# Moving the product of two weight matrices behind the attention, with its loads on another queue

## The chip, the cores and the metric

The kernel runs on one core of a Trainium2 chip. The time is the device time of one execution in microseconds (us), lower is better: the median of 3 executions of the kernel before is 733.92 us (733.58 to 734.43).

## The reference, cut to what matters

```python
# q, k, v: (4, 12, 448, 64); x below: (1792, 768)
scores = q @ k.T / sqrt(64) - log(448)
x = sigmoid(scores) @ v                            # heads joined to 768 columns
h = max(x @ w1, x @ w2, x @ w3)                    # three 768 x 768 matrices
x = h @ w_out                                      # 768 x 768
h = x @ w_in                                       # 768 x 1024
s = h * softmax(h)
out = layernorm(s) * g_ln @ w_out2                 # 1024 x 768
```

All in float32; the weights come as 64-bit floats.

## The kernel before, in words

**Precision.** TensorE works in a reduced float32 format, so most operands are split in a high part (a cast) and a low part (what the cast left, helper `rest`, L56), and each product is three matmuls: high x high, high x low, low x high. Only the product of attention weights and v (L300) takes plain float32.

**Folding two matrices.** There is nothing between `w_out` (wo) and `w_in` (wi), so the kernel computes W = wo x wi itself (`gen_w`, L242): 12 groups of 18 matmuls, 512 columns each, into a PSUM tile `pw`. ACT and DVE split each result into a tile `ws`, and GpSimd's queue (POOL) writes it to DRAM (`w_d`, L258), from where it is read back late (`wf`, L399).

**Preparing weights.** One unit is 128 x 768 doubles. `load_next` (L132) loads it into one of two `raw` buffers, on SyncE's queue (SP). `prepare` (L163) turns it into float32 (ACT L147, DVE L150 and L153), asks for the next load, then makes the high part (ACT, L51) and the low part (DVE, L56). wi lies whole in SBUF (`wip`); units of wo and w1 to w3 go through a ring of three slots (`ring`). The program text puts these operations in a list of background work, and `run_bg(n)` emits the next n of them. 11 units are needed before W can be finished that far (`first`: 8 of wi, 3 of wo).

**Attention.** 24 pairs of heads. For a pair: `load_qk` and `load_v` (SP), `prep_qk` splits q and k (four DVE operations), `scores` makes four blocks c = 0..3 (six matmuls each, two at a time in the two halves of the array's rows, L281, then one sigmoid on ACT, L289), and `attend` multiplies the four blocks with v (L300; the trace counts two matmuls for each in the text) and splits the result into `xh` (ACT) and `xl` (DVE). The text runs `attend` one pair behind `scores`.

**Order.** Only TensorE's order is that of the text. For ACT, DVE, POOL and SP a planner in the compiler walks the program in its own modelled time and lets each engine take the earliest instruction of the text whose inputs and buffers are then free; the resulting order is fixed, and each engine runs it strictly in sequence.

**W between the pairs.** From pair 4 on, `fill(9)` puts half a group of W behind each pair (L329), in a single PSUM bank (`ps_f`); what is left runs after the last pair (L332). PSUM has eight banks: six for scores, one for `av`, one for `pw`.

**What follows.** `layer1` (tile `pg`, 72 groups of 18 matmuls, 448 columns: 1296), then by 128 tokens `layer2` with W (tile `h`, L426, 512 columns, 504 matmuls) and `output` (tile `po`, L502, 384 columns, 672 matmuls).

**Where the tiles lie.** SBUF is laid out from the left (const, ring, wip, apool and, once these are closed, h, w2, wf, hsplit) and from the right (x, raw, tp). In the program of before the bytes within a partition are: ring 1728 and wi 20160 (both multiples of 64), hh 161472, wf 112320 and w2 63168 (multiples of 64 too), kt 81344 and qt 89536 (multiples of 64); xh 143328 and, for `output`, lh 206816 lie 32 past a multiple of 64. The second tiles of each kind keep these remainders.

Of the kernel before, what the change touches and what calls it, by code (L numbers as in the profile page):

```python
# [7 lines left out]
F32 = mybir.dt.float32  # L8
F32R = mybir.dt.float32r
# [4 lines left out]
PSUM = bass.MemoryType.PSUM  # L14
DRAM = bass.MemoryType.DRAM

P = 128
B, H, S, D = 4, 12, 448, 64
SX = S + D
# [9 lines left out]
U = 768  # L29
NG = 3 * FC  # L30
RAWS = 2
WARM = 4


def sigmoid_attention_max_moe_solu_ln(tc, q, k, v, w123, wo, wi, w2, g, out):
# [13 lines left out]
    def copy(eng, dst, src):  # L49
        if eng is act:  # L50
            act.copy(dst, src)  # L51
        else:
            eng.tensor_copy(dst, src)
# [4 lines left out]
    def open_pool(name, bufs, side="left", space=None):  # L58
        kw = dict(name=name, bufs=bufs, side=side)
        if space is not None:  # L60
            kw["space"] = space
        cm = tc.tile_pool(**kw)
        return cm, cm.__enter__()

    def shut(*cms):
        for cm in cms:
            cm.__exit__(None, None, None)
# [2 lines left out]
    order.__enter__()  # L70
    dr_cm, dram = open_pool("dram", 1, space=DRAM)
    c_cm, const = open_pool("const", 1)
    r_cm, ring = open_pool("ring", 3)
    x_cms, xps = [], []
    for b in reversed(range(B)):
        cm, p = open_pool(f"xp{b}", 1, side="right")
# [2 lines left out]
    raw_cm, rawp = open_pool("rawp", 2, side="right")  # L79
    wi_cm, wip = open_pool("wip", 1)  # L80
    a_cm, apool = open_pool("apool", 2)
    ps1 = [open_pool("ps_sc", 3, space=PSUM), open_pool("ps_av", 1, space=PSUM), open_pool("ps_f", 1, space=PSUM)]
    ps_sc, ps_av, ps_f = (p for _, p in ps1)

    ident = const.tile([P, P], F32, name="ident")
    bias_s = const.tile([P, 1], F32, name="bias_s")
# [10 lines left out]
    def run_bg(n=1):  # L97
        while n > 0 and bg:
            if next(bg[0], "end") == "end":
                bg.popleft()  # L100
            else:
                n -= 1
# [20 lines left out]
    def source(key):  # L123
        if key[0] == "wi":
            return wi[key[1], key[2]]
        if key[0] == "wo":
            return wo[key[1]]
        if key[0] == "w2":
            return w2[key[1]]
        return w123[key[1]]  # L130

    def load_next():  # L132
        i = state["load"]
        if i >= len(stream):
            return
        state["load"] += 1
        key = stream[i]
        t = rawp.tile([P, U, 2], I32, tag="raw", name=f"raw{i}", bufs=RAWS)
        sp.dma_start(out=t, in_=source(key).rearrange("p (n t) -> p n t", t=2))
        raws[key] = t  # L140

    def to_f32(raw, y):
# [20 lines left out]
    def prepare(key):  # L163

        raw = raws.pop(key)
        y = rawp.tile([P, U], F32, tag="y", name="y_" + "_".join(map(str, key)), bufs=2)
        for op in to_f32(raw, y):
            op()
            yield
        load_next()  # L170
        if key[0] == "wi":
            _, n, i = key
            if i % 2 == 0:
                wis[(n, i // 2)] = [wip.tile([P, 2 * U], F32R, name=f"wi{p}{n}_{i}") for p in ("h", "l")]
            hi, lo = (t[:, (i % 2) * U : (i % 2 + 1) * U] for t in wis[(n, i // 2)])
        elif key[0] == "w2":
            kc = key[1]
            act.activation(y, y, AF.Copy, scale=g_sb[:, kc : kc + 1])
            yield
            hi, lo = w2t["h"][:, kc], w2t["l"][:, kc]  # L180
        else:
            slot = ring.tile([P, 2, U], F32R, tag="ring", name="r_" + "_".join(map(str, key)))
            slots[key] = slot
            hi, lo = slot[:, 0], slot[:, 1]
        copy(act, hi, y)
        yield
        rest(dve, lo, y, hi)
        ready.add(key)
        yield
# [16 lines left out]
    def load_qk(pr):  # L206
        if pr >= NP:
            return
        kr = apool.tile([P, SX], F32, tag="kr", name=f"kr{pr}", bufs=1)
        qr = apool.tile([P, S], F32, tag="qr", name=f"qr{pr}", bufs=1)  # L210
        sp.dma_start(out=kr, in_=k[pr])
        sp.dma_start(out=qr, in_=q[pr])
        qk_raw[pr] = (qr, kr)

    def load_v(pr):
        if pr >= NP:
            return
        vr = apool.tile([P, 2, 4, D], F32, tag="vr", name=f"vr{pr}", bufs=2)
        sp.dma_start(out=vr, in_=v[pr])
        v_ops[pr] = vr  # L220

    def prep_qk(pr):
        if pr >= NP:
            return
        qr, kr = qk_raw.pop(pr)
        kt = apool.tile([P, 2, SX], F32R, tag="kt", name=f"kt{pr}")
        qt = apool.tile([P, 2, S], F32R, tag="qt", name=f"qt{pr}")
        qk_ops[pr] = (qt, kt)
        copy(dve, kt[:, 0], kr)
        copy(dve, qt[:, 0], qr)  # L230
        rest(dve, kt[:, 1], kr, kt[:, 0])
        rest(dve, qt[:, 1], qr, qt[:, 0])
        load_qk(pr + 1)


    def group(ps, terms):
# [5 lines left out]
    def gen_w():  # L242
        for n, fc in groups:
            need(("wo", fc))
            for i in range(4):
                need(("wi", n, i))
            wo_s = slots[("wo", fc)]
            ps = ps_f.tile([P, 512], F32, tag="f", name=f"pw{n}_{fc}")
            terms = []
            for kc in range(KC):  # L250
                lh, ll = (wo_s[:, i, kc * P : (kc + 1) * P] for i in range(2))
                rh, rl = (t[:, (kc % 3) * 512 : (kc % 3 + 1) * 512] for t in wis[(n, kc // 3)])
                terms += [(lh, rh), (lh, rl), (ll, rh)]
            yield from group(ps, terms)
            s = wip.tile([P, 2, 512], F32R, tag="ws", name=f"ws{n}_{fc}", bufs=1)
            copy(act, s[:, 0], ps)
            rest(dve, s[:, 1], ps, s[:, 0])
            pool.dma_start(out=w_d[:, fc, :, n * 512 : (n + 1) * 512], in_=s.bitcast(F32))  # L258
            if n == 1:
                slots.pop(("wo", fc))  # L260
                queue_unit(stream[len(first) + fc])

    filler = gen_w()

    def fill(n):
        for _ in range(n):
            if next(filler, "end") == "end":
                return


    xs_hi, xs_lo, hts = {}, {}, {}
    weights = {}
# [1 line left out]
    def scores(pr, c):  # L274
        qt, kt = qk_ops[pr]
        sc = ps_sc.tile([P, 2, 512], F32, tag="sc", name=f"sc{pr}_{c}")
        terms = ((0, 0), (0, 1), (1, 0))
        for t, (x, y) in enumerate(terms):
            for j in range(2):
                rows = slice(j * D, (j + 1) * D)  # L280
                pe.matmul(  # L281
                    sc[:, j, :S],
                    lhsT=kt[rows, x, c * P : (c + 1) * P],
                    rhs=qt[rows, y],
                    start=(t == 0),
                    stop=(t == len(terms) - 1),
                )
        sf = apool.tile([P, 2, S], F32, tag="sf", name=f"sf{pr}_{c}", bufs=7)
        act.activation(sf, sc[:, :, :S], AF.Sigmoid, bias=bias_s, scale=1.0 / math.sqrt(D))  # L289
        weights[(pr, c)] = sf  # L290

    def attend(pr):

        b, hp = divmod(pr, NPAIR)
        vr = v_ops.pop(pr)
        pa = ps_av.tile([P, 512], F32, tag="av", name=f"av{pr}")
        for c in range(4):
            sf = weights.pop((pr, c))
            for j in range(2):
                pe.matmul(pa[j * D : (j + 1) * D, :S], lhsT=vr[:, j, c], rhs=sf[:, j], start=(c == 0), stop=(c == 3))  # L300
        if hp == 0:
            xs_hi[b] = xps[b].tile([P, KC, S], F32R, name=f"xh{b}")
            xs_lo[b] = xps[b].tile([P, KC, S], F32R, name=f"xl{b}")
        copy(act, xs_hi[b][:, hp], pa[:, :S])
        rest(dve, xs_lo[b][:, hp], pa[:, :S], xs_hi[b][:, hp])
        load_v(pr + 2)


    act.preload_act_table_set("sigmoid_and_others")
    load_qk(0)  # L310
    load_v(0)
    load_next()
    load_next()
    prep_qk(0)
    load_v(1)
    sp.dma_start(out=g_sb, in_=g)
    for key in first:
        queue_unit(key)
    for pr in range(NP + 1):
        if pr < NP:  # L320
            for c in range(4):
                scores(pr, c)
                if c == 1:
                    prep_qk(pr + 1)
                run_bg(1)
        if pr > 0:
            attend(pr - 1)
            run_bg(2)
        if WARM <= pr < NP:  # L329
            fill(9)  # L330
        run_bg(2)
    while next(filler, "end") != "end":  # L332
        pass
    for cm, _ in reversed(ps1):
        shut(cm)
    shut(a_cm, wi_cm)


    h_cm, hpool = open_pool("hpool", 1)
    w2_cm, w2p = open_pool("w2p", 1)  # L340
    psg_cm, ps_g = open_pool("ps_g", 4, space=PSUM)
    w2t["h"], w2t["l"] = (w2p.tile([P, K2, DM], F32R, name=f"w2{p}") for p in "hl")
    hts = [hpool.tile([P, NT], F32, name=f"h{f}") for f in range(FC)]
    tick = [0]
# [231 lines left out]
```

## Time and profile before

| | before |
|---|---|
| median of 3 executions | 733.92 us |
| the profiled execution | 736.76 us, its span 734.8 us |
| PE busy in the span | 708.0 us (96%) |
| DVE busy | 318.7 us (43%) |
| ACT busy | 264.9 us (36%) |
| mean granted clock of TensorE | 0.995 |
| moved by DMA | 80.81 MB |

The span runs from the first to the last instruction of the profiled execution. A busy PE is not yet a PE at its peak: matmuls overlap, and one that waits or runs at a slow pace still counts as busy. So the pace from start to start is read beside the busy time. W and attention end at 228.97 us of the span, `layer1` at 496.81 us, and the rest belongs to `layer2` and `output`.

### The profile page before, as it was taken

To read this page: it belongs to the slowest core of one execution; us is meant where nothing else is said; L and a number is where in the kernel's file an instruction comes from. 1 tells how busy PE (TensorE), PEld (TensorE's weight loads), DVE (VectorE), ACT (ScalarE), POOL (GpSimd) and SP (SyncE) were. 2 spreads that over 40 slices of the span, in tenths; PEclk is the share of its full clock that TensorE was granted. 3 is DMA by queue.
4 is the path that set the end of the run, shared out by engine and by line. 5 is a ranking of instruction groups with operands and counts; after the bars stand their busy time and mean duration, and the time that the engine had idled before them with its cause. 6 is when DMAs were issued, how large, how long until landed. Compare 5 with 4: busy or idle time off the path is not lost.

```text
span 734.8 us, 9063 instructions
## 1 busy us (share of the span) xinstructions
PE 708.0 (96%) x3664; PEld 574.9 (78%) x3664; DVE 318.7 (43%) x578; ACT 264.9 (36%) x428; POOL 9.6 (1%) x19
## 2 busy tenths in 40 slices
PE   5887999999999999999999999999999999999998
PEld 3344555555557999999999999997999999999997
DVE  4875345343422243533532131214954455555540
ACT  5875566555652123333330110101422223232221
POOL 0000000000000000000000000000000000000000
PEclk9999999999999999999999999999999999999999
DMA  7887344453324122333231000710132222222231
GB/s 242 280 269 258 118 154 154 124 176 118 128 72 144 43 87 87 128 106 110 86 114 60 1 0 1 295 48 1 58 114 94 98 90 79 79 79 79 79 101 44
DMA packets 29706, 80.81 MB, mean 110 GB/s; under 512 B 3424, under 2 KB 12896, under 8 KB 28896
## 3 DMA queue, kind: packets, MB, share of 16 engines
q1 hardware_dynamic: 27936, 73.94, 29.9%
q0 software_dynamic: 1728, 6.29, 2.2%
q8 instruction: 29, 0.48, 0.3%
q14 instruction: 13, 0.11, 0.0%
HBM read 62.13 MB, written 18.09 MB: 109 GB/s over the span
## 4 chain that ended last, share of the span: by engine, by line
PE 89%; DMA 5%; ACT 4%; issue 1%; DVE 0%; SPq 0%; ACTq 0%
PE pg L239 36%; PE po L502 16%; PE h L426 16%; PE av L300 8%; PE pw L239 7%; PE sc L281 6%; DMA raw<-in_wo 3%; DMA raw<-in_wi 2%; ACT sf L289 2%; ACT y_wo L147 1%; ACT ws L51 0%; ACT y_wi L147 0%; ACT wih L51 0%; PE pt L486 0%; DVE wil L56 0%
## 5 line engine op out<-in xcount | busy, mean ns | idle before, releaser
L239 PE MATMUL pg<-xh,r_w 128*128 128x448 f32 x864 | 249.0, 369 | 0.0
L239 PEld LDWEIGHTS pg<-xh,r_w 128*128 128x128 f32 x864 | 162.4, 188 | 16.3
L239 PE MATMUL pg<-xl,r_w 128*128 128x448 f32 x432 | 159.4, 369 | 0.0
L426 PE MATMUL h<-wf,hh 128*128 128x512 f32 x336 | 103.9, 390 | 0.8 <-issue 0.8
L289 ACT ACTIVATE sf<-sc,bias_s 128x896 f32<-128x896 f32 x96 | 92.0, 1007 | 28.6 <-PE sc L281 25.3
L281 PE MATMUL sc<-qt,kt 64*128 64x448 f32 x576 | 75.4, 399 | 21.0 <-ACT sf L289 14.1
L239 PEld LDWEIGHTS pg<-xl,r_w 128*128 128x128 f32 x432 | 81.2, 188 | 7.9
L281 PEld LDWEIGHTS sc<-qt,kt 64*128 64x128 f32 x576 | 53.6, 196 | 42.8 <-ACT sf L289 26.3
L300 PE MATMUL av<-sf,vr 128*64 128x448 f32 x384 | 80.2, 561 | 0.0
L502 PE MATMUL po<-w2h,lh 128*128 128x384 f32 x224 | 75.4, 336 | 0.0
L502 PE MATMUL po<-w2h,ll 128*128 128x384 f32 x224 | 75.3, 336 | 0.0
L502 PE MATMUL po<-w2l,lh 128*128 128x384 f32 x224 | 75.3, 336 | 0.0
L364 DVE TENSOR_TENSOR h<-pg,h 128x448 f32<-128x448 f32 x48 | 29.9, 624 | 102.9 <-PE pg L239 102.9
L426 PEld LDWEIGHTS h<-wf,hh 128*128 128x128 f32 x336 | 62.8, 188 | 13.4 <-issue 1.1
L426 PE MATMUL h<-wf,hl 128*128 128x512 f32 x168 | 65.6, 390 | 0.0
L300 PEld LDWEIGHTS av<-sf,vr 128*64 128x64 f32 x384 | 26.1, 140 | 43.1 <-issue 42.2
L438 DVE TENSOR_REDUCE st<-h 128x1 f32<-128x1024 f32 x14 | 17.1, 1223 | 85.1 <-PE h L426 85.1
L239 PE MATMUL pw<-wih,r_wo 128*128 128x512 f32 x144 | 50.8, 409 | 1.4 <-DVE ws L56 1.4
L51 ACT CAST hh<-h 128x128 fp32r<-128x128 f32 x84 | 18.1, 295 | 93.6 <-PE h L426 86.7
L51 ACT CAST r_w<-y_w 128x768 fp32r<-128x768 f32 x18 | 15.1, 839 | 93.3 <-PE pg L239 93.3
L239 PEld LDWEIGHTS pw<-wih,r_wo 128*128 128x128 f32 x144 | 27.0, 187 | 21.9 <-issue 11.3
L502 PEld LDWEIGHTS po<-w2l,lh 128*128 128x128 f32 x224 | 42.1, 188 | 0.6
(65 smaller groups left out, 606.7 us busy)
## 6 DMA issues: line engine op xcount, KB each, us to landing
raw<-in_w SPq DMA_DIRECT2D x26, 768.0 KB, 4.3
kr<-in_k SPq DMA_DIRECT2D x24, 256.0 KB, 2.8
vr<-in_v SPq DMA_DIRECT2D x24, 256.0 KB, 3.2
raw<-in_wi SPq DMA_DIRECT2D x8, 768.0 KB, 5.8
w_d<-ws POOLq DMA_DIRECT2D x12, 512.0 KB, 3.2
wf<-w_d SPq DMA_DIRECT2D x6, 1024.0 KB, 10.0
u_d<-ub SPq DMA_DIRECT2D x12, 512.0 KB, 3.0
ut<-u_d SPq DMA_DIRECT2D x48, 128.0 KB, 3.1
```

The source lines that it names most:

```text
L51: act.copy(dst, src)
L147: act.activation(y, raw.bitcast(F32)[:, :, 1], AF.Prelu, scale=2.0**-112, alpha=2.0**32)
L239: pe.matmul(ps, lhsT=l, rhs=r, start=(i == 0), stop=(i == n - 1))
L281: pe.matmul(sc[:, j, :S], lhsT=kt[rows, x, c * P : (c + 1) * P], rhs=qt[rows, y], start=(t == 0), stop=(t == len(terms) - 1),)
L289: act.activation(sf, sc[:, :, :S], AF.Sigmoid, bias=bias_s, scale=1.0 / math.sqrt(D))
L300: pe.matmul(pa[j * D : (j + 1) * D, :S], lhsT=vr[:, j, c], rhs=sf[:, j], start=(c == 0), stop=(c == 3))
L364: dve.tensor_tensor(out=hv, in0=ps[:, :S], in1=hv, op=ALU.max)
L426: pe.matmul(ps[:, n], lhsT=l, rhs=r, start=(f == 0 and i == 0), stop=(f == FC - 1 and i == 2))
L438: dve.tensor_reduce(out=nmax, in_=ps, axis=AX.XY, op=ALU.max, negate=True)
L502: pe.matmul(ps[:, :hw], lhsT=l, rhs=r, start=(kc == 0 and i == 0), stop=(kc == K2 - 1 and i == 2))
```

## The change

W's groups leave the attention: `fill` and `WARM` go, and all 12 groups run after the last pair, each in one of four PSUM banks (the pool `ps_g` that `layer1` uses too), with two `ws` buffers. Every fourth matmul emits one background operation there.

The freed bank goes to `av`, which has two. `attend` is cut by blocks: behind the scores of a pair come blocks 2 and 3 of the pair before and blocks 0 and 1 of this pair.

The raw weights are loaded from POOL's queue, and the text asks for the first two with pair 1 (`load_next`) and emits three background operations for each pair from pair 2 on. The high part of wi, wo and w1 to w3 is cast by DVE in place of ACT.

q and k have two buffers each and are loaded two pairs ahead, v has three; the buffers for attention weights (`sf`) go from 7 to 6. A pad of 32 bytes in `const` shifts everything that is laid out from the left by 32 bytes.

```diff
     c_cm, const = open_pool("const", 1)
+    const.tile([P, 8], F32, name="pad")
...
-    ps1 = [open_pool("ps_sc", 3, space=PSUM), open_pool("ps_av", 1, space=PSUM), open_pool("ps_f", 1, space=PSUM)]
+    ps1 = [open_pool("ps_sc", 3, space=PSUM), open_pool("ps_av", 2, space=PSUM)]
...
-        sp.dma_start(out=t, in_=source(key).rearrange("p (n t) -> p n t", t=2))
+        pool.dma_start(out=t, in_=source(key).rearrange("p (n t) -> p n t", t=2))
...
-        copy(act, hi, y)
+        copy(act if key[0] == "w2" else dve, hi, y)
...
-        kr = apool.tile([P, SX], F32, tag="kr", name=f"kr{pr}", bufs=1)
-        qr = apool.tile([P, S], F32, tag="qr", name=f"qr{pr}", bufs=1)
+        kr = apool.tile([P, SX], F32, tag="kr", name=f"kr{pr}", bufs=2)
+        qr = apool.tile([P, S], F32, tag="qr", name=f"qr{pr}", bufs=2)
...
-        load_qk(pr + 1)
+        load_qk(pr + 2)
...
-            s = wip.tile([P, 2, 512], F32R, tag="ws", name=f"ws{n}_{fc}", bufs=1)
+            s = wsp.tile([P, 2, 512], F32R, tag="ws", name=f"ws{n}_{fc}", bufs=2)
...
+    for pr in range(2):
+        load_qk(pr)
+        load_v(pr)
+    load_v(2)
     prep_qk(0)
...
+    for pr in range(NP):
+        if pr == 1:
+            load_next()
+            load_next()
+        for c in range(4):
+            scores(pr, c)
+            if c == 1:
+                prep_qk(pr + 1)
+        if pr > 1:
+            run_bg(1)
         if pr > 0:
-            attend(pr - 1)
-            run_bg(2)
-        if WARM <= pr < NP:
-            fill(9)
-        run_bg(2)
-    while next(filler, "end") != "end":
-        pass
+            attend(pr - 1, 2)
+            attend(pr - 1, 3)
+        if pr > 1:
+            run_bg(1)
+        attend(pr, 0)
+        attend(pr, 1)
+        if pr > 1:
+            run_bg(1)
+    attend(NP - 1, 2)
+    attend(NP - 1, 3)
+    run_bg(1 << 20)
...
+    psg_cm, ps_g = open_pool("ps_g", 4, space=PSUM)
+    ws_cm, wsp = open_pool("wsp", 2)
+    for i, _ in enumerate(gen_w()):
+        if i % 4 == 3:
+            run_bg()
+    shut(ws_cm, wi_cm)
```

## Rows read from the trace of the kernel before

**Rows 1.** Stretches: length; busy PE, PEld, DVE, ACT, POOL (count); clock; DMA share, GB/s.
```profile
4.98:73.84 68.86, 53.94 (x291) 29.71 (x291) 48.26 (x77) 48.18 (x59) 0.84 (x1) 0.95 0.80 269
73.84:207.45 133.61, 132.50 (x787) 76.46 (x786) 53.15 (x96) 79.90 (x96) 5.84 (x8) 1.00 0.43 139
...
228.97:496.81 267.84, 267.84 (x1296) 243.30 (x1295) 87.60 (x128) 63.71 (x92) 0.74 (x1) 1.00 0.24 85
```

**Rows 2.** The chain that ended last, share of the span by line.
```profile
by line: PE pg L239 36.4%; PE po L502 15.9%; PE h L426 15.7%; PE av L300 8.3%; PE pw L239 6.8%; PE sc L281 5.8%; DMA raw<-in_wo 2.8%; DMA raw<-in_wi 2.5%; ACT sf L289 1.9%; issue 0.6%; ACT y_wo L147 0.5%; ACT ws L51 0.5%; ACT y_wi L147 0.4%
```

**Rows 3.** Waits from 4.98 to 73.84 us: total us, times, longest.
```profile
PEld sc L281 <- ACT sf L289: 19.8, 11, 4.3
PE sc L281 <- ACT sf L289: 13.0, 6, 3.9
ACT y_wi L147 <- DMA raw<-in_wi: 10.6, 3, 7.2
```

**Rows 4.** ACT's first two entries in the order of time: start, us.
```profile
9.27 0.89 ACT L147 ACTIVATE y_wi<-raw 128x768 f32<-128x768 f32 x1 [7.25 <-DMA raw<-in_wi]
10.06 1.90 ACT L289 ACTIVATE sf<-sc,bias_s 128x896 f32<-128x896 f32 x2
```

**Rows 5.** The chain in order of time, pieces of it: start us, us, what.
```profile
124.13 2.78 PE sc L281 x24
126.91 3.16 PE av L300 x16
130.07 2.27 PE pw L239 x9
132.34 2.85 PE sc L281 x24
...
182.35 0.59 ACT ws L51
...
223.23 0.59 ACT ws L51
...
223.85 0.70 DVE ws L56
...
224.59 4.37 PE pw L239 x18
228.97 267.84 PE pg L239 x1296
...
523.26 8.33 PE po L502 x48
531.59 8.21 PE h L426 x36
```

**Rows 6.** Tile `raw`, whole run: duration min/median/max ns, first to last start.
```profile
L147 ACT ACTIVATE y_w<-raw x26: 890/902/921, 117.9 to 424.7; 128x768 f32<-128x768 f32 x26
```

**Rows 7.** Groups of instructions from 4.98 to 73.84 us: busy us, mean ns, idle before.
```profile
L53 DVE CAST kt<-kr 128x512 fp32r<-128x512 f32 x8 | 3.4, 425 | 2.4 <-DMA kr<-in_k 1.5 <-PE sc L281 0.8
...
L289 ACT ACTIVATE sf<-sc,bias_s 128x896 f32<-128x896 f32 x28 | 27.2, 1007 | 2.5 <-PE av L300 1.4 <-PE sc L281 1.0
...
L51 ACT CAST wih<-y_wi 128x768 fp32r<-128x768 f32 x8 | 6.7, 833 | 0.9 <-DVE y_wi L153 0.9
```

**Rows 8.** What SP's queue waited for, up to 74 us: total us, times, longest.
```profile
SPq L211 <- DVE kt L56: 15.0, 8, 2.6
```

**Rows 9.** Tile `w_d`, whole run: POOL's issues, and its DMAs from issue to landing.
```profile
L258 POOL DMA_DIRECT2D w_d<-ws x12: 727/727/844, 66.1 to 230.7; - x12
...
DMA to landing us min/median/max: 3.1/3.2/15.8
```

**Rows 10.** Tile `raw` up to 74 us: its DMAs from issue to landing.
```profile
DMA to landing us min/median/max: 4.2/5.8/8.5
```

**Rows 11.** PE in order of time, pair 23: two score matmuls that start together, twice.
```profile
208.10 0.37 PE L281 MATMUL sc<-qt,kt 64*128 64x448 f32 x2
...
208.93 0.37 PE L281 MATMUL sc<-qt,kt 64*128 64x448 f32 x2
```

More of the change, by code (lines that the diff above doesn't have):

```diff
@@ L31 @@
 RAWS = 2
-WARM = 4
 def sigmoid_attention_max_moe_solu_ln(tc, q, k, v, w123, wo, wi, w2, g, out):
@@ L81, in sigmoid_attention_max_moe_solu_ln @@
     a_cm, apool = open_pool("apool", 2)
-    ps1 = [open_pool("ps_sc", 3, space=PSUM), open_pool("ps_av", 1, space=PSUM), open_pool("ps_f", 1, space=PSUM)]
-    ps_sc, ps_av, ps_f = (p for _, p in ps1)
+    ps1 = [open_pool("ps_sc", 3, space=PSUM), open_pool("ps_av", 2, space=PSUM)]
+    ps_sc, ps_av = (p for _, p in ps1)
     ident = const.tile([P, P], F32, name="ident")
@@ L217, in load_v @@
             return
-        vr = apool.tile([P, 2, 4, D], F32, tag="vr", name=f"vr{pr}", bufs=2)
+        vr = apool.tile([P, 2, 4, D], F32, tag="vr", name=f"vr{pr}", bufs=3)
         sp.dma_start(out=vr, in_=v[pr])
@@ L247, in gen_w @@
             wo_s = slots[("wo", fc)]
-            ps = ps_f.tile([P, 512], F32, tag="f", name=f"pw{n}_{fc}")
+            ps = ps_g.tile([P, 512], F32, tag="g", name=f"pw{n}_{fc}")
             terms = []
@@ L261, in gen_w @@
                 queue_unit(stream[len(first) + fc])
[L263 to L268, printed above, removed]
     xs_hi, xs_lo, hts = {}, {}, {}
@@ L287, in scores, with attend @@
                 )
-        sf = apool.tile([P, 2, S], F32, tag="sf", name=f"sf{pr}_{c}", bufs=7)
+        sf = apool.tile([P, 2, S], F32, tag="sf", name=f"sf{pr}_{c}", bufs=6)
         act.activation(sf, sc[:, :, :S], AF.Sigmoid, bias=bias_s, scale=1.0 / math.sqrt(D))
         weights[(pr, c)] = sf
-    def attend(pr):
+    pas = {}
+    def attend(pr, c):
         b, hp = divmod(pr, NPAIR)
[L295 to L300, printed above, removed]
+        vr = v_ops[pr]
+        if c == 0:
+            pas[pr] = ps_av.tile([P, 512], F32, tag="av", name=f"av{pr}")
+        pa = pas[pr]
+        sf = weights.pop((pr, c))
+        for j in range(2):
+            pe.matmul(pa[j * D : (j + 1) * D, :S], lhsT=vr[:, j, c], rhs=sf[:, j], start=(c == 0), stop=(c == 3))
+        if c < 3:
+            return
+        pas.pop(pr)
+        v_ops.pop(pr)
         if hp == 0:
@@ L305, in attend @@
         rest(dve, xs_lo[b][:, hp], pa[:, :S], xs_hi[b][:, hp])
-        load_v(pr + 2)
+        load_v(pr + 3)
     act.preload_act_table_set("sigmoid_and_others")
[L310 to L313, printed above, removed]
+    for pr in range(2):
+        load_qk(pr)
+        load_v(pr)
+    load_v(2)
     prep_qk(0)
-    load_v(1)
     sp.dma_start(out=g_sb, in_=g)
@@ L318, in sigmoid_attention_max_moe_solu_ln @@
         queue_unit(key)
[L319 to L325, printed above, removed]
-        if pr > 0:
-            attend(pr - 1)
-            run_bg(2)
-        if WARM <= pr < NP:
-            fill(9)
-        run_bg(2)
-    while next(filler, "end") != "end":
-        pass
+    for pr in range(NP):
[8 more added lines that the diff above has]
+            run_bg(1)
+        if pr > 0:
+            attend(pr - 1, 2)
[9 more added lines that the diff above has]
+    run_bg(1 << 20)
     for cm, _ in reversed(ps1):
         shut(cm)
-    shut(a_cm, wi_cm)
+    shut(a_cm)
+    psg_cm, ps_g = open_pool("ps_g", 4, space=PSUM)
[4 more added lines that the diff above has]
+    shut(ws_cm, wi_cm)
     h_cm, hpool = open_pool("hpool", 1)
     w2_cm, w2p = open_pool("w2p", 1)
-    psg_cm, ps_g = open_pool("ps_g", 4, space=PSUM)
     w2t["h"], w2t["l"] = (w2p.tile([P, K2, DM], F32R, name=f"w2{p}") for p in "hl")
```

## The prediction, made before the change was run

> **What bounds the kernel now.** I read the stretches first. From 73.84 us on PE is busy 99% of the time and in `layer1` all of it, at the full clock; DVE, ACT and the DMA engines have room there [rows 1]. Only the stretch from 4.98 to 73.84 us differs: PE 53.94 of 68.86 us, DVE and ACT 48 us each, the DMA engines 0.80 busy at 269 GB/s. The chain that ended last says the same for the whole span: four fifths of it are matmuls, and of the rest the loads of raw wo and wi are the largest, 2.8% + 2.5% of 734.8 us = 38.9 us [rows 2]. The waits of the early stretch show how a load reaches PE: the scores waited 19.8 + 13.0 us for sigmoids, while ACT waited for raw weights [rows 3]. ACT's first two entries are the pattern: a weight conversion stands ahead of the first sigmoid and holds ACT for 7.25 us until its load lands [rows 4]. So PE's sum bounds the kernel, and the early stretch, with three resources at 70 to 80% and fixed orders between them, adds about 20 us to it.
>
> **Attention and W, step by step.** In the steady part a pair costs 2.85 us of scores and 3.16 us of the product with v, with 2.27 us of W behind it [rows 5]. Without W it is 6.01 us; 24 pairs take 144.2 us. W's 216 matmuls of 512 columns go at the pace of `h`, which has the same width: 8.21 / 36 = 0.228 us [rows 5], 49.3 us. Together 193.5 us of PE work, whatever the order. Before, this part ends at 228.97 us [rows 5], so 35.5 us are lost, in three places:
> - 4.98 us until the first matmul. The same loads and the same four DVE operations stand before it; I leave it.
> - The early stretch: 7 pairs (42.1 us) and three half groups of W (6.8 us) in 68.86 us: 20.0 us.
> - The rest, 10.5 us. Each nine matmuls of W between two pairs cost 2.27 and not 2.05 us; one PSUM bank makes PE wait for ACT's 0.59 and DVE's 0.70 us (224.59 - 223.23 = 1.4 us near the end); and at 182.35 us, say, the next pair's sigmoid stands behind W's copy [rows 5].
>
> The third item nearly goes: W in one piece over four banks has 3 x 4.1 us to empty a bank, against 1.3 us of work. I keep 0.5 us for the switches.
>
> The second item decides, and the text's own pacing (three operations a pair, from pair 2) does not settle it, since the order of ACT, DVE and POOL is the planner's. How far it pulls work up can be read: the first unit of w1 to w3 is put on the list behind W's eighth group, which ended at 182.35 us [rows 5], but ACT converted it at 117.9 us [rows 6], 64 us earlier. The first two loads need nothing, and POOL is idle, so I expect them in the first 2 us and the units after them as early as buffers allow, among the first eight or so pairs, much as now.
>
> What such an early stretch costs I bound from rows. Above: as now, less the three half groups, 68.86 - 6.8 = 62.1 us for 7 pairs. Below: the DMA engines never idle, 0.80 x 68.86 = 55.1 us [rows 1]. DVE's sum gives the same: its 48.26 us [rows 1] and 11 casts that it takes over. Each is 425 ns x 768 / 512 = 0.64 us by its cast of k, a gift of 0.83 us to ACT [rows 7]: 48.3 + 7.0 = 55.3 us. ACT falls to 48.2 - 9.2 = 39 us, so its sigmoids (1.0 us, four a pair [rows 7]) have more room; and SP no longer holds a load of k behind a single buffer, which cost its queue 15.0 us [rows 8]. Less 42.1 us of PE work this is a loss of 13 to 20 us. I take 17: DVE and DMA together leave little slack, and a conversion ahead of a sigmoid still waits for its load. If the order follows the text instead, 55 operations are spread over 18 pairs, DVE and ACT fit under 6.01 us, and about 3 us are lost: the mean granted clock of the early stretch is 0.95, 5% of 62 us [rows 1].
>
> So the part ends at 4.98 + 17 + 193.5 + 0.5 = 216.0 us in place of 228.97: **13.0 us less**.
>
> **Edits at nothing.** Third v buffer, second `av` bank, `attend` by blocks: the matmuls are the same and in the steady part the product never waits for a sigmoid; its cover is ACT, 4 x 1.0 us of sigmoids within 6.01 us. If ACT were late by one conversion (0.9 us), PE would stand still for what exceeds that room. Six `sf` buffers: three fit a pair that is consumed within the next. The units wo 3 to 5 and w 0 to 2, which are converted during W, have at least two groups (8.2 us) each; were one late, `layer1` would start late by that much. DVE's casts during `layer1` lie beside 87.6 busy us of 267.84 [rows 1].
>
> **The loads on POOL's queue.** They queue with W's write-back. POOL's 12 issues took 727 ns in the middle and 844 at most, and a write of 512 KB landed after 3.2 us [rows 9]; SP's loads of 768 KB landed after 5.8 us in the crowded stretch [rows 10]. Scaled by size, POOL's 3.2 us is 4.8. So the row gives no lateness, and with it the queue is priced at nothing; the other end is POOL's longest landing, 15.8 us [rows 9], and the last rival covers it.
>
> The Trainium skill, "SBUF — State Buffer", section "SBUF: two separate sides", speaks against this part: descriptors of a GpSimd DMA are written through a port that a float32 copy on VectorE locks, so the DMA seems blocked by the copy. Rows 9 show issues of nearly one length, though DVE ran many such copies; the rule's case is the last rival below.
>
> **The pad.** From start to start `layer1` needs 267.84 / 1296 = 206.7 ns for 448 columns, `h` 228.1 ns for 512, `po` 8.33 / 48 = 173.5 ns for 384 [rows 5]. The granted clock is the full one, 2.4 GHz of its two levels [rows 1], so the columns alone take 186.7, 213.3 and 160.0 ns, and what is over is 20.0, 14.7 and 13.5 ns. `layer1` alone reads stationary operands at a multiple of 64 bytes against moving ones 32 past it; `h` has both at a multiple, and `po` the reverse. The pad gives `layer1` equal remainders. If the unequal ones cost it the difference, the pace becomes 186.7 + 14.1 = 200.8 ns: 1296 x 5.9 = **7.6 us less**. Against it: scores, also 448 columns and with equal remainders, go at (208.93 - 208.10) / 4 = 207 ns a step [rows 11], though with two matmuls at once. No row tests the new placing itself. The bounds are 7.6 us less and, if a moving operand 32 past a multiple costs this by itself, the same 5.9 ns on W, `h` and `po`, whose moving operands all shift: 1392 x 5.9 = 8.2 us more. I take the gain, as three shapes of four have the short gap and equal remainders are the common case there.
>
> **The sum.** Profiled execution 736.76 - 13.0 - 7.6 = 716.2 us. That execution lies 2.84 us above the median shown, so the forecast is **713 us**.
>
> **Rivals.**
> - *The order follows the text* (loss 3 us in place of 17). For: a planner that sees DVE full would leave conversions for later pairs. Against: rows 6. Part 1 is then 27.0 us, the time 699 with the pad's gain and 707 without. Chance 0.27.
> - *The pad does nothing* (the step of 207 ns belongs to 448 columns). For: rows 11. Against: the other widths' gaps. Early order: 721 us. Chance 0.23.
> - *The moving operand's place alone costs.* `po`, with its stationary operand 32 past and its moving one at a multiple, has the smallest gap, which speaks for it; that scores are slow with neither shifted, against. 721 + 8 = 729 us. Chance 0.08; for a quarter of it the early stretch gains so little that the time is no longer faster.
> - *Slower: POOL's loads land late.* The place is ACT's queue, where a conversion holds all sigmoids behind it. 13 loads lie there; each that lands later by d holds PE by up to d. It decides from 13 x d = 20.6 us (what the parts above give), d = 1.6 us. With d = 2.7 us, by which SP's longest landing of 8.5 us exceeds its middle one [rows 10], it is 35 us, and the kernel takes 748. For: conversions wait for loads already [rows 3]. Against: rows 9. Chance 0.06. The rule cited above would work in this way, with DVE's new casts as the lock.
>
> **Numbers.** My forecast has 0.36. A difference of 0.2% (1.5 us) is about what a measurement of this kernel can tell from no change. Faster: 0.36 + 0.27 + 0.23 and three quarters of 0.08, 0.92. Same 0.02. Slower 0.06. The range from 699 to 725 leaves out the last two rivals and the lower half of what lies around 699, some 0.2; it holds the bounds of the early stretch (loss 13 to 20, so 709 to 716) with and without the pad's gain.
>
> **What would show it.** `layer1` starts near 216 us; before that no `pw` stands between pairs, and after the last pair 216 of them run at 228 ns without a wait for `ws`. POOL issues raw loads within the first 2 us and ACT's conversions of wi stand among the first eight pairs; if they begin after pair 2 at 6.01 us a pair, the first rival is right. `layer1`'s 1296 matmuls take 260 us, 268 if the pad does nothing; `h` and `po` at 234 and 179 ns would mean the third rival. Raw loads with a median landing over 7 us would mean the last. The forecast is wrong outright if `layer1` starts later than 222 us or W waits for wo's units.

## The result, and the profile after

The changed kernel takes **723.84 us** (median of 4 executions, 720.19 to 726.94) against 733.75 for the kernel before in the same comparison (732.19 to 734.43). The ratio is 0.9866, 95% interval 0.9817 to 0.9915. The forecast was 713 us: the sign and the range held, but the gain is 9.9 us and not 20.6. The profiled execution took 724.43 us with a span of 722.7 us. Against the profiled one of before (736.76) it gained 12.3 us, in two places: `layer1` starts 7.1 us sooner (221.84 in place of 228.97), where 13.0 had been forecast, and is 5.2 us shorter (262.65 in place of 267.84), where 7.6 had been forecast. What follows `layer1` is as long as before (238.2 us against 238.0).

Stretches of the changed kernel, answering to [rows 1]: up to the steady pairs, the steady pairs, W, `layer1`. Columns: stretch, length, busy us (count) of PE, PEld, DVE, ACT, POOL, granted clock, DMA share, GB/s.

```profile
4.95:69.21 64.26, 49.50 (x274) 24.86 (x274) 50.22 (x85) 39.13 (x47) 8.06 (x12) 0.89 0.76 263
69.21:172.63 103.42, 103.42 (x689) 54.40 (x689) 40.44 (x80) 71.06 (x86) 0.54 (x1) 1.00 0.37 118
172.63:221.84 49.21, 49.21 (x218) 40.74 (x218) 22.97 (x32) 11.50 (x17) 10.71 (x16) 1.00 0.51 185
221.84:484.49 262.65, 262.65 (x1296) 243.04 (x1295) 95.64 (x144) 50.78 (x76) 11.37 (x21) 1.00 0.25 89
```

From 69.21 us to the end of `layer1` PE has no gap, and the granted clock is 1.00. What is lost lies in the first stretch: 7 pairs in 64.26 us, where the forecast counted 42.1 us of work, so by its count **22.2 us are lost and not 17**.

That count takes seven products with v for seven pairs, and the number of matmuls shows that it is too high. Before, `attend` ran a pair behind: the 291 matmuls of [rows 1] are 7 x 24 of scores, 27 of W and 96 of products, so six products. In the changed kernel half of a pair's product runs a pair sooner: 274 matmuls are 168 of scores and 104 of products, six and a half, and two at the edge. With the pieces of [rows 5] the work was 19.95 + 18.96 + 6.8 = 45.7 us before and is 19.95 + 20.54 = 40.5 us now. So **23.1 us were lost before and 23.8 us are lost now**: the early stretch gained nothing. DVE is busy for 78% of it, the DMA engines for 76% and ACT for 61%, and the granted clock is 0.89.

The chain that ended last in the changed kernel, pieces of it in order of time (start us, us, what), answering to [rows 2, 5].

```profile
28.18 5.49 PE av L295 x16
...
38.63 4.88 DMA raw<-in_wi
...
46.31 4.85 PE av L295 x16
...
55.56 6.13 DMA raw<-in_wo
...
65.11 4.10 PE av L295 x16
...
72.08 3.16 PE av L295 x16
...
172.63 49.20 PE pw L239 x216
221.84 262.65 PE pg L239 x1296
...
510.89 8.35 PE po L512 x48
```

Two things are to be seen in the early part. Loads of raw weights are on the path that PE waits for. And the same 16 matmuls of `av` that take 3.16 us at the full clock take 5.49, 4.85 and 4.10 us. The granted clock in these three pieces was 0.57, 0.65 and 0.77: TensorE ran partly at the lower of its two levels (1.2 in place of 2.4 GHz). The three are 4.96 us longer than three at full clock.

The waits of the changed kernel from 4.95 to 69.21 us (total us, times, longest), answering to [rows 3].

```profile
PE sc L273 <- ACT sf L281: 14.4, 7, 4.1
...
ACT y_wi L147 <- DMA raw<-in_wi: 12.2, 5, 6.7
...
ACT y_wo L147 <- DMA raw<-in_wo: 10.3, 5, 3.0
...
DVE kt L52 <- DMA kr<-in_k: 6.0, 1, 6.0
```

The pattern is the one of before: scores wait for sigmoids, and ACT, which would make them, waits for raw weights: for wi 12.2 us, where [rows 3] showed 10.6.

### The profile page after: what moved, and what is told of

It reads as the page before. It is cut to its first block, busy times and chain, and to the rows that moved or that the text cites. A ratio compares the mean times of both kernels' runs of the same rounds, so it can differ in the third digit from the quotient of the medians.

```text
span 722.7 us, 9080 instructions
## 1 busy us (share of the span) xinstructions
PE 698.5 (97%) x3664; PEld 576.0 (80%) x3664; DVE 334.0 (46%) x610; ACT 237.7 (33%) x396; POOL 32.6 (5%) x59
## 4 chain that ended last, share of the span: by engine, by line
PE 93%; DMA 3%; DVE 1%; issue 1%; ACT 1%; SPq 0%; ACTq 0%
PE pg L239 36%; PE po L512 16%; PE h L436 16%; PE av L295 10%; PE sc L273 8%; PE pw L239 7%; DMA kr<-in_k 1%; ACT sf L281 1%; DMA raw<-in_wo 1%; DMA raw<-in_wi 1%; DVE y_wi L153 0%; PE pt L496 0%; DVE qt L55 0%; DVE y_wi L150 0%; DVE kt L55 0%
## 5 line engine op out<-in xcount | busy, mean ns | idle before, releaser
L239 PE MATMUL pg<-xh,r_w 128*128 128x448 f32 x864 | 245.5, 365 | 0.0
L239 PE MATMUL pg<-xl,r_w 128*128 128x448 f32 x432 | 157.8, 365 | 0.0
L281 ACT ACTIVATE sf<-sc,bias_s 128x896 f32<-128x896 f32 x96 | 88.9, 1006 | 31.4 <-PE sc L273 31.4
L273 PE MATMUL sc<-qt,kt 64*128 64x448 f32 x576 | 73.8, 392 | 19.7 <-ACT sf L281 14.4
L295 PE MATMUL av<-sf,vr 128*64 128x448 f32 x384 | 82.4, 574 | 0.0
L147 ACT ACTIVATE y_w<-raw 128x768 f32<-128x768 f32 x26 | 23.3, 897 | 100.3 <-DVE r_w L55 93.2
L239 PE MATMUL pw<-wih,r_wo 128*128 128x512 f32 x144 | 44.6, 390 | 0.0
L372 ACT COPY h<-pg 128x448 f32<-128x448 f32 x24 | 12.8, 533 | 92.3 <-PE pg L239 92.3
L512 PEld LDWEIGHTS po<-w2h,lh 128*128 128x128 f32 x224 | 42.1, 188 | 0.5
```

Of the source, the lines that this page charges most:

```text
L147: act.activation(y, raw.bitcast(F32)[:, :, 1], AF.Prelu, scale=2.0**-112, alpha=2.0**32)
L239: pe.matmul(ps, lhsT=l, rhs=r, start=(i == 0), stop=(i == n - 1))
L273: pe.matmul(sc[:, j, :S], lhsT=kt[rows, x, c * P : (c + 1) * P], rhs=qt[rows, y], start=(t == 0), stop=(t == len(terms) - 1),)
L372: act.copy(hv, ps[:, :S])
L512: pe.matmul(ps[:, :hw], lhsT=l, rhs=r, start=(kc == 0 and i == 0), stop=(kc == K2 - 1 and i == 2))
```

## The experiments

Diffs are against the changed kernel, except where the kernel before is named. Every ratio is to the kernel before, run on the same chip.

### The order of the text, on four engines, then on ACT alone

The first theory put the loss down to the planner's order: weight conversions stand ahead of the sigmoids that PE waits for. The rival: DVE and the DMA engines have too much to do in the early stretch, so that another order gives nothing.

```diff
+    ET = mybir.EngineType
+    text = tc.manual_schedule(engines={ET.Activation, ET.DVE, ET.Pool, ET.SP})
+    text.__enter__()
     act.preload_act_table_set("sigmoid_and_others")
...
     run_bg(1 << 20)
+    text.__exit__(None, None, None)
```

> Only the order of ACT, DVE, POOL and SP during the attention changes: it is that of the program text, so conversions start behind pair 2's scores, one unit per 1.7 pairs. Theory A (the early stretch is lost because the planner puts two conversions per pair ahead of the next pair's first sigmoid, and each waits for its load): the pairs run at 6.0 us from pair 2 on, layer1 starts at 201 to 206 us in place of 221.84, time 703 to 708. Rival B (the early stretch is bound by the sums of DMA bytes and DVE work, which stay the same): the loss only moves to later pairs, layer1 starts at 215 to 222, time 717 to 724.

It took 706.26 us, ratio 0.9625 (0.9606 to 0.9643). The chain of this run, pieces in order of time:

```profile
2.11 10.28 DMA kr<-in_k
...
14.43 2.65 PE sc L273 x17
...
20.23 2.83 PE sc L273 x24
...
204.10 262.65 PE pg L239 x1296
```

From pair 1 on, pairs follow each other at 6.0 us, but for one wait of 1.2 us near 125 us, and `layer1` starts 17.7 us sooner than in the changed kernel. The rival falls: the loads and DVE's work are the same in sum, and the loss does not come back in later pairs. Most of what is still lost is the start: the second k, loaded from 2.11 us on, lands at 12.38.

The second run holds only ACT to the text (`engines={ET.Activation}`).

> Only ACT runs in the order of the text during the attention; DVE, POOL and SP are the planner's. Theory A1 (the loss sits in ACT's order, since a load that is late there holds the sigmoids): layer1 starts within 2 us of the 204.1 us of the run with all four in text order, time 705 to 709. Rival A2 (DVE's order is what counts, since conversions there delay the split of the next q and k): most of the loss stays, layer1 starts above 212 us.

It took 707.17 us, ratio 0.9639 (0.9606 to 0.9672), and `layer1` starts at 204.28 us. So ACT's order alone, with everything else left to the planner, takes nearly all of the loss away. The order changes two things at once: where in a pair a conversion stands, and how many conversions fall into the early pairs. Up to 69 us ACT converts 13 units in the changed kernel and 5 in this run. No run holds one of the two still. In the order of time, ACT of the changed kernel around the longest wait of PE (start us, us, instruction, [idle before it and what ended that]):

```profile
59.52 0.90 ACT L147 ACTIVATE y_wo<-raw 128x768 f32<-128x768 f32 x1 [2.96 <-DMA raw<-in_wo]
60.32 0.51 ACT L50 CAST xh<-av 128x448 fp32r<-128x448 f32 x1
61.77 0.91 ACT L147 ACTIVATE y_wo<-raw 128x768 f32<-128x768 f32 x1 [0.94 <-DMA raw<-in_wo]
62.57 3.69 ACT L281 ACTIVATE sf<-sc,bias_s 128x896 f32<-128x896 f32 x4
```

And PE beside it:

```profile
57.88 2.09 PE L273 MATMUL sc<-qt,kt 64*128 64x448 f32 x18
63.62 1.49 PE L273 MATMUL sc<-qt,kt 64*128 64x448 f32 x6 [3.65 <-ACT sf L281]
65.04 4.17 PE L295 MATMUL av<-sf,vr 128*64 128x448 f32 x16
```

Three score blocks are there at 59.97 us, which fills the three PSUM buffers. The four sigmoids come in one row behind *two* conversions, each of which waits for its load; the fourth block must wait for the first sigmoid to free a buffer. PE stands still for 3.65 us, and the product behind it runs slow. With ACT in the order of the text a conversion follows the four sigmoids instead and waits in time that nobody needs:

```profile
39.09 3.70 ACT L281 ACTIVATE sf<-sc,bias_s 128x896 f32<-128x896 f32 x4 [1.83 <-PE sc L273]
42.73 0.53 ACT L50 CAST xh<-av 128x448 fp32r<-128x448 f32 x1
43.16 0.94 ACT L147 ACTIVATE y_wi<-raw 128x768 f32<-128x768 f32 x1
```

Now ACT waits for PE, and not the reverse.

### A third raw buffer, and the cast back on ACT

If conversions wait because a load is only asked for when the one before is converted, a third buffer helps.

```diff
-RAWS = 2
+RAWS = 3
...
-        sf = apool.tile([P, 2, S], F32, tag="sf", name=f"sf{pr}_{c}", bufs=6)
+        sf = apool.tile([P, 2, S], F32, tag="sf", name=f"sf{pr}_{c}", bufs=5)
```

> A third buffer for raw weights (and five sf buffers in place of six, for room). Theory A says that ACT waits for a load because a buffer, and so the load, is released only one conversion earlier: with a third buffer loads are issued earlier, ACT's waits for raw weights (22.5 us before 69 us) fall to under 10, and layer1 starts at 212 to 218. If DMA bytes bind (rival B), the waits stay near 20 us and layer1 starts at 219 to 223.

It took 719.76 us, ratio 0.9809 (0.9789 to 0.9829); `layer1` starts at 217.53 us, 4.3 sooner. ACT's waits for raw weights fell as expected, from 12.2 + 10.3 = 22.5 us to 8.8, and 7.5 of these stand ahead of the first sigmoid. But most of the loss stayed. In front of its conversions ACT now waited 12.1 us for DVE (4.2 in the changed kernel), which works on the same units and on q and k, and PE still waited 10.9 us for sigmoids, where it had been 14.4. The planner's order came out another way too, with sigmoids between most conversions. So late loads alone are not the loss.

The next run makes the high part of the weights on ACT again, which separates ACT's load from DVE's.

```diff
-        copy(act if key[0] == "w2" else dve, hi, y)
+        copy(act, hi, y)
```

> The changed kernel with the high part of all weights cast on ACT again, as before (planner's order kept). The theory that the early stretch is lost to what stands ahead of the sigmoids on ACT: 11 casts of 0.83 us more on ACT, some of them ahead of a sigmoid, so layer1 starts later than 221.84 us by 1 to 9 us, time 725 to 733. The rival that DVE binds the early stretch: 11 x 0.65 us less on DVE, layer1 starts up to 7 us earlier, time 717 to 723.

It took 726.05 us, ratio 0.991 (0.9888 to 0.9932), and `layer1` starts at 223.24 us, 1.4 later, at the low end of what the first theory expected. Up to the steady pairs DVE had 3.4 us less to do (46.86 in place of 50.22) and ACT 8.0 more (47.08 in place of 39.13). The gain of up to 7 us that the rival expected did not come, so less work on DVE with more on ACT frees nothing. Whether the move of the casts is worth anything can't be told: 1.4 us is less than the scatter of the changed kernel's executions, 720.19 to 726.94, and the two intervals overlap.

### The queue of the loads

```diff
-        pool.dma_start(out=t, in_=source(key).rearrange("p (n t) -> p n t", t=2))
+        sp.dma_start(out=t, in_=source(key).rearrange("p (n t) -> p n t", t=2))
```

> The changed kernel with the raw weights loaded by SP again. If POOL's queue itself is late (descriptors, locks by DVE's copies), loads land sooner, below 4.9 us in the middle, and the early stretch shortens for that reason. If the queue costs nothing, the landing times are as with POOL (4.8 to 5.9 us) and what changes is only the order that the planner finds: the early stretch then differs by the place of the conversions among the sigmoids, 64.3 us give or take 8.

In the planner's order it changes nothing: 724.59 us, ratio 0.9873 (0.9845 to 0.9902), `layer1` at 222.66. From issue to landing (min/median/max), first the changed kernel, tile `raw` up to 74 us, answering to [rows 10]:

```profile
DMA to landing us min/median/max: 4.3/4.9/9.0
```

and the same with the loads on SP:

```profile
DMA to landing us min/median/max: 4.2/6.0/8.4
```

So POOL's queue is not late. This run shows one thing more. The planner put ACT's order another way here, in most pairs with a sigmoid between the two conversions (start us, us, instruction, [idle before it and what ended that]):

```profile
39.09 0.92 ACT L147 ACTIVATE y_wo<-raw 128x768 f32<-128x768 f32 x1 [2.77 <-DMA raw<-in_wo]
39.90 1.00 ACT L281 ACTIVATE sf<-sc,bias_s 128x896 f32<-128x896 f32 x1
...
41.84 0.92 ACT L147 ACTIVATE y_wi<-raw 128x768 f32<-128x768 f32 x1 [0.52 <-DMA raw<-in_wi]
42.66 2.79 ACT L281 ACTIVATE sf<-sc,bias_s 128x896 f32<-128x896 f32 x3
```

The time is the same. That both conversions of a pair stand ahead of all four sigmoids is therefore not what makes the loss; one ahead of three sigmoids and one ahead of the fourth cost as much.

With the order of the text the queue does matter:

> All four in text order, and the raw weights on SP's queue, where the first two then stand behind the loads of pairs 0 to 3. In the run with POOL the first raw loads started at 1.3 us, the second k landed at 12.4 us and pair 1's scores began at 14.4 us. If these two loads took the bandwidth from k, k now lands before 8 us, pair 1 begins at 9.5 to 11 us and layer1 at 199 to 202 us, time 701 to 704. If k's landing does not depend on them, layer1 stays at 204 us and the time at 706; if SP's queue holds loads back (a raw load behind a load of v that waits for its buffer), ACT waits for raw weights and the time is above 707.

It took 709.96 us, ratio 0.9678 (0.965 to 0.9706), 3.7 us more than with the loads on POOL. Two of its waits up to 155 us show why:

```profile
ACT y_wo L147 <- DMA raw<-in_wo: 4.8, 1, 4.8
PE sc L273 <- ACT sf L281: 4.5, 1, 4.5
```

One raw load came late enough for ACT to wait 4.8 us for it, ahead of a sigmoid, and PE stood for 4.5 us. Its buffer was free at 116.39 us, when DVE had finished with the unit in it, but SP issued it at 118.57 us, behind the loads of a k and a q that waited for DVE, and it landed 6.5 us later. In a strict order SP's queue holds a raw load behind loads that wait for their buffers: up to 155 us, its loads of k waited 56.0 us for `kt` and its loads of v 37.8 us for `av`. But its start was better: pair 1's scores ran at 12.48 us in place of 14.43, as no raw load shared the first microseconds with the second k.

That gave the next version: the order of the text, loads on POOL, but the first two only after the second k has been converted. A copy of eight columns on POOL, into the pad, holds them (besides the lines for the order of the text):

```diff
         if pr == 1:
+            pool.tensor_copy(out=pad, in_=qk_ops[1][1][:, 0, 0:8].bitcast(F32))
             load_next()
             load_next()
```

> As e1_text_order, and a copy of 8 columns on POOL that reads pair 1's split k stands ahead of the first raw load, so that the raw loads leave the second k alone. If the start loss that e1 still has is the shared bandwidth of the first loads: pair 1's scores start near 12.5 us in place of 14.4, layer1 near 202.2 us in place of 204.1, time 704 to 705 us. If the raw loads, now some 6 us later, make the first conversions late instead, or if the second k is late for a reason of its own (SP's queue): layer1 starts at 204 us or later, time 706 or more.

It took **704.25 us** (703.93 to 705.11), ratio 0.9617 (0.9599 to 0.9635): the best version, 19.6 us below the changed kernel. By the ratios it can't be told from the plain order of the text, whose interval overlaps; the traces show the difference. Its chain:

```profile
11.85 2.78 PE sc L273 x23
...
17.80 2.83 PE sc L273 x24
...
201.54 262.65 PE pg L239 x1296
```

Pair 1 runs 2.6 us sooner than in the run with the plain order of the text, and all of it arrives at `layer1`. PE is busy 54.66 of the 55.05 us from 4.95 to 60 us.

### Where the product of the two matrices stood before

Was the forecast's upper bound for the early stretch sound? It took the 6.8 us of W's three half groups off its length. If PE would have waited in that time anyway, they were free, and the bound was too low. The kernel before, with W behind the last pair and nothing else changed:

```diff
-WARM = 4
+WARM = 24
```

> The kernel before with W's groups moved behind the last pair and nothing else (one bank, everything on its old queue and engine). It tests the upper bound that the forecast took for the early stretch: 68.86 us less 6.8 us of W's three half groups. Theory: those half groups lay in time in which PE would have waited for sigmoids anyway, so that without them the same 7 pairs still need 66 to 70 us from the first matmul (end near 71 to 75 us, now 73.84), with longer waits for sigmoids. Rival, as the forecast had it: the half groups were on PE's path, and the 7 pairs end near 67 us or before. Behind the early stretch pairs at 6.0 us, then 12 groups in one bank at 4.1 us and 1.4 us of emptying each: layer1 starts near 240 us by the theory, near 235 by the rival; time 742 to 750.

It took 748.26 us, ratio 1.0187 (1.0157 to 1.0217). Its chain, around the start of pair 7 and of `layer1`:

```profile
61.62 4.33 PE av L300 x16
65.95 2.79 PE sc L281 x21
...
236.10 4.38 PE pw L239 x18
240.48 267.84 PE pg L239 x1296
```

Pair 7's scores start at 65.95 us in place of 73.84 [rows 1]: 7.9 us sooner. The half groups were on PE's path, and the forecast's bound was fair for the old order of ACT; the theory of free half groups falls. (That `layer1` starts at 240.48, as that theory had it, comes from the rest: with one bank a group takes 236.10 + 4.38 - 230.33 - 4.39 = 5.8 us and not the 5.5 of the expectation, and the last product and a wait of PE lie in between.) So without W this kernel spends 65.95 - 5.00 = 61.0 us on 7 pairs, counted from its first matmul, and the changed kernel 64.26. Half of that difference is work: there are six products in the first stretch and six and a half in the second, 1.6 us more. The work here is 38.9 us, so 22.1 us are lost, against 23.1 in the kernel before and 23.8 in the changed one. The 1.7 us between this run and the changed kernel are less than the scatter of the changed kernel's executions (720.19 to 726.94). In the planner's order the stretch lost about as much with the old text as with the new one.

### The pad

```diff
-    const.tile([P, 8], F32, name="pad")
```

> The changed kernel without its 32-byte pad. If the pad is what brought layer1 from 267.8 to 262.7 us, layer1 is back at 267.8 us, with h, po and W within 1 us of what they are, and the kernel is 5 us slower (729). If layer1's gain came from something else (fewer loads beside it, DVE's casts), it stays at 262.7 and the time at 724.

It took 728.52 us, ratio 0.993 (0.9903 to 0.9957). The reverse, the pad alone in the kernel before:

> The kernel before with the pad alone, nothing else. If the pad's gain comes from equal remainders of the two operands of layer1 and is independent of the other parts: layer1 takes 262.6 to 262.7 us in place of 267.84, all else stays, and the time is 5.2 us less than before, 728 to 729 us (ratio 0.993). If the pad helps only together with the other parts, or moves something else (bank, order of the planner), the time lies outside 727 to 731.

It took 729.06 us, ratio 0.9935 (0.9909 to 0.9961). `layer1` without the pad, in the chain of the first of the two:

```profile
220.22 267.84 PE pg L238 x1296
```

and with it, in the chain of the second:

```profile
228.39 262.65 PE pg L240 x1296
```

The pad is worth 5.2 us of `layer1` with or without the rest of the change. (In the first of these runs `layer1` starts 1.6 us sooner than in the changed kernel, 220.22 against 221.84, so the profiled executions differ by 3.5 us; the medians differ by 4.7.)

What does the 32 bytes' work? Moving x, at the right end, by 32 bytes in place of the tiles at the left puts both operands at a multiple of 64:

```diff
-    const.tile([P, 8], F32, name="pad")
+    rp_cm, rpad = open_pool("rpad", 1, side="right")
+    rpad.tile([P, 8], F32, name="rpad_t")
...
```

> No pad in const, but everything laid out from the right is shifted by 32 bytes: layer1 has stationary and moving operands both at a multiple of 64 bytes. If equal remainders are what helps, layer1 takes 262.7 us as in the changed kernel; if the stationary operand's place 32 past a multiple helps by itself, 267.8 us as before.

Moving both sides gives `layer1` unequal remainders again, with the places exchanged:

> Pad in const and the shift from the right: layer1 has the stationary operand 32 past a multiple of 64 and the moving one at a multiple, as the output stage of the kernel before; the output stage has them the other way round, as layer1 before. If equal remainders are what helps, layer1 takes 267.8 us; if the moving operand at a multiple helps, 262.7 us or less (259.2 at the smallest gap of 13.3 ns). If the placing of layer1 before is bad at every width, the output stage's step of 48 matmuls rises from 8.34 to 8.6 us.

Lines of the chain, x alone moved (one execution, 723.81 us):

```profile
221.19 262.65 PE pg L240 x1296
...
510.26 8.34 PE po L513 x48
```

and both sides moved (one execution, 728.65 us):

```profile
222.09 264.96 PE pg L241 x1296
...
513.46 8.48 PE po L514 x48
```

Steps from these lines, the time over the count, by the remainders of the two operands over a multiple of 64 bytes:

| stationary, moving | 448 columns (`layer1`) | 384 columns (`output`) |
|---|---|---|
| 0, 32 | 206.7 ns (before) | 176.7 ns (both moved) |
| 32, 0 | 204.4 ns (both moved) | 173.5 ns (before) |
| 32, 32 | 202.7 ns (changed) | 174.0 ns (changed) |
| 0, 0 | 202.7 ns (x moved) | 173.8 ns (x moved) |

A stationary operand at a multiple against a moving one 32 past it is the slow case at both widths. The reverse costs 1.8 ns at 448 columns and nothing at 384; the expectation for both sides moved had 267.8 us or at most 262.7 for `layer1`, and the 264.96 lie between. Where the remainders are equal, it does not matter which they are.

## Why the forecast missed, step by step

**Right.** W in one piece over four banks: 49.20 us (49.3 forecast), 228 ns a matmul without a wait between groups. The first matmul at 4.95 us. The raw loads leave POOL at 1.32 and 2.31 us, about as early as expected, and ACT's conversions of wi stand among the first eight pairs. W's late units are never waited for. `po` and `h` keep their pace within 0.5 ns, so the rival of the moving operand alone falls, as does the one in which the pad does nothing.

**Right, with a wrong count.** The third item of the loss went, as forecast, but it was smaller: one product of 3.16 us stood in it as loss, so that it was 7.3 us and not 10.5. Now the 17 pairs take 103.42 us, against 17 x 2.85 + 17.5 x 3.16 = 103.75 us of work: nothing is lost. The early stretch was given the same 3.16 us as work that is not in it.

**Wrong: the loss of the early stretch**, 17 us in the forecast with bounds 13 and 20, 22.2 measured by its own count, and 23.1 before against 23.8 after by the number of matmuls. The step that failed is the choice of 17, by which the stretch would lose 3 us less than before: it drew the loss down towards a lower bound made of busy times, 55.1 us of the DMA engines and 55.3 us of DVE, "DVE and DMA together leave little slack". DVE had 50.22 us of work and not 55.3, and the stretch still took 64.26. Less work on DVE freed nothing, the queue of the loads changed nothing, and with ACT alone in the order of the text `layer1` started 17.6 us sooner. What held PE was the sigmoids on ACT, behind conversions that waited for loads and, where the loads were sooner, for DVE. The forecast said that a conversion ahead of a sigmoid still waits for its load, but gave this no price; its middle took 3 us off the loss all the same. The upper bound was nearly met: 62.1 us hold six products, with the half product more they are 63.7, and 64.26 were measured. Part of the loss is the clock: a gap of PE was followed by a product at the lower clock, 4.96 us in three places of the chain, for which the sum had no term of its own. The start of `layer1` at 221.84 us is just short of the 222 us at which the forecast called itself wrong outright.

**Wrong in size: the pad.** The mechanism was right, equal remainders are what helps. The term was 1296 x 5.9 ns = 7.6 us; measured 1296 x 4.0 ns = 5.2. It took the gap of the other widths, 14.1 ns over the columns, for one of 448 columns, which keeps 202.7 - 186.7 = 16.0. The row of the scores, which the forecast set against itself, had shown a wide gap at 448 columns with equal remainders [rows 11].

**The rivals.** "The order follows the text" is not what the planner made of this change. With the order held to the text and the first loads delayed `layer1` starts at 201.54 us, and the rival had 27.0 us less, so 202.0. That its price fits is in part luck: its 3 us of loss were a clock of 0.95, but in that run the granted clock is 1.00 up to 60 us, and what is lost is the wait before pair 1 and one wait near 120 us. "POOL's loads land late" falls: median landing 4.9 us. The Trainium skill, "SBUF — State Buffer", section "SBUF: two separate sides", has VectorE's float32 copies hold up the descriptors of GpSimd's DMAs. This trace agrees in kind: of POOL's 15 issues of raw loads up to 74 us, six took 0.60 to 0.97 us, and each of them ended 0.11 to 0.13 us behind the end of a cast on DVE; the others took 0.53 to 0.66 us, three of them beside a cast too. But the price was 0.44 us an issue at most, and the loads still landed sooner than from SP's queue (4.9 us in the middle against 6.0), so it moved nothing.

**What stays open.** Which part of ACT's order makes the loss: that conversions stand ahead of sigmoids, or that 13 of them fall into the early pairs. Why the planner orders ACT as it does was not tried either; `attend` by blocks, the new buffers and the text's places for background work changed together. And why steps of 448 columns take the remainders so.

## What to carry to other kernels

An engine that is 60% busy can bind by its order alone: look in its order of time for work that isn't urgent, that waits for a load, and that stands ahead of what the bound engine needs. Price each such wait, with the row of the load or of the engine that it waits for, and add what the clock loses behind a gap; a sum of busy times gives neither. And count the matmuls of a stretch before calling the rest of it loss. Before believing a share of busy time to be the limit, hold one engine to the order of the text: here that was worth 16.7 us on ACT (723.84 - 707.17), more than the change itself.

## What was unexpected in the hardware

- The place of an operand within 64 bytes changes the pace of a matmul: 206.7 or 202.7 ns at 448 columns, 176.7 or 173.5 ns at 384, as the table shows.
- In the changed kernel, behind gaps of 2.4 to 4.1 us of PE, 16 matmuls took 4.10 to 5.49 us in place of 3.16. The length of the gap alone does not decide it: in the kernel before with late W, a product behind a gap of 2.73 us took its usual time, and one behind 2.34 us took 4.33. The granted clock of the slowest product shows it (columns as above):

```profile
28.18:33.66 5.48, 5.48 (x18) 1.71 (x18) 4.35 (x9) 2.46 (x4) 0.91 (x1) 0.57 0.83 287
```

- Two raw loads of 768 KB, asked for at 1.3 and 2.3 us, shared the first microseconds with a k of 256 KB, which landed at 12.38 us; with them behind it, DVE could convert that k at 7.11 us, and pair 1's scores ran 2.6 us sooner.
